# A fused attention, soft MoE and product layer on one Trainium2 core: one instruction plan for all queues, the last batch pair by pair, and memory handed on in blocks

## The chip, the cores and the metric

The kernel runs on one core of a Trainium2 chip. The metric is the device time of one execution in microseconds. The core has TensorE (PE), VectorE (DVE), ScalarE (ACT), GpSimd (POOL) and SyncE (SP), which here issues nearly all DMAs.

## The reference

```python
# attention, 8 batches x 8 heads, 576 tokens, head dimension 64; block-causal mask with blocks of 64
scores = scale * np.matmul(q, k.transpose(0, 1, 3, 2))
scores = np.where(block_i >= block_j, scores, -1e9)
attn = softmax(scores); x = attn @ v            # x becomes 4608 x 512
# soft MoE, 8 experts with 4 slots each (32 slots)
logits = x @ phi
slot_input = softmax(logits, over tokens).T @ x
slot_out[e] = np.maximum(slot_input[e] @ w1[e], 0) @ w2[e]      # w1: 512 x 1024, w2: 1024 x 512
y = softmax(logits, over slots) @ slot_out
# product layer
h = (y @ u1) * (y @ u2) @ w3                    # u1, u2: 512 x 1024, w3: 1024 x 1024
out = h @ w_out                                 # 1024 x 512
```

## The kernel before, in words

*Attention.* Heads are worked in 32 pairs (`n`), four to a batch, eight batches (`b`). For a pair, raw q and k are loaded (`op_ld`) and split into a high part (ACT, `op_cast`) and a low part (POOL, `op_sub`); a first product on TensorE (`op_M`, L360) gives block maxima by VectorE (`op_R`, L364), which a transposition and a DMA bring to a row; then come the scores (`op_Q`, L400), their exponentials on ACT (`op_E`), sums on POOL (`op_P`, for the last pair partly on VectorE) and TensorE (`op_SU`, L449), and the product with v (`op_V`, L433). After four pairs of a batch the sums are inverted and spread by DMA, x is scaled on POOL (`op_sx`), and the batch's logits, maxima, exponentials and its share of the slot inputs follow (`op_lg` to `op_SSu`). Between these, 26 pieces of 64-bit weights (`op_b`) are converted to 32 bits: w_out, the first row of w3, u1 and u2.

*What sets the order.* `Plan` (L74) lists every operation with its engine, a duration, what it waits for, PSUM banks and a due time (`OFF`, `EARLY`); `order()` plays it forward, with a look-ahead per engine (`LOOK`, `WAIT`), and returns one order. In the attention all five queues are issued in that order by hand (`manual_schedule`, L801).

*The last batch.* `push_tail` (L629) writes the chain of batch 7 after the plan: transposed sums, logits, their transpositions and reductions (`logit_t`, L664), natural x (`x_nat`, L707), dispatch maxima and exponentials (`disp_max`), slot inputs (`slot_in`, `slot_sum`, `slot_share`, `slot_T`, L737). Between the steps `fill` issues matmuls of zeros (`warm`, L42; `WARM` gives 10, 11, 16 and more). Batch 6's last steps (`S`, `cT`) are moved into this chain (`late`).

*Experts and joined weight.* `Rest.run` (L899) multiplies w3 and w_out into one weight W (8 row blocks of 24 matmuls, `w_rows`, L930), with each operand split into two terms: 192 matmuls. Pieces of w3 are loaded and converted (`convert`, `narrow`, `split`). For each expert: first layer (L1020), copy, transposition, relu, second layer (L1048); expert weights come in 16 halves of 2 MB through five windows (`load_expert`), four of them loaded late in attention. `w_steps` puts a listed number of W matmuls (`MM`) between the expert's steps. Only PE and SP are in hand order here (`MAN`); other queues are put in order by the framework. All this starts after the slot inputs: the high parts of w_out wait for `keep["shared"]` (L991).

*H and the last stage.* The experts' output is multiplied with u1 and u2 (L1089) and transposed; slot products (`slot_products`, L1108) are made on VectorE, with three small ones on POOL (L1125), and multiplied with W to H (`h_chunk`, L1131). `final` (L1173) goes over 12 groups of 384 tokens: products of combine weights (VectorE, ACT, POOL), then three tiles of 13 matmuls with H (L1238), a copy and a store.

*Memory.* Each stage opens pools and closes them; a pool of the next stage lies where an earlier one was.

Of the kernel before, what the change touches and what calls it, by code (L numbers as in the profile page):

```python
# [21 lines left out]
W3B = 4  # L22
ROT = 2
MAN = ('SP', 'PE')
ORDERED = ('PE', 'DVE', 'Activation', 'Pool', 'SP')
FIN = (7, 11, 11)
W3_AT = (0, 1, 2, 3, 4, 5, 6, 7)
SEQ = 1
WARM = (6, 10, 11, 0, 16, 0, 0, 0)
WF = 25  # L30
AHEAD = 36
HP = False
CT = (1, 2)
STEPS = 28
MM = (0, 5, 4, 13, 5, 4, 14, 5, 4, 13, 5, 4, 14, 5, 4, 13, 5, 4, 14, 5, 4, 14, 5, 4, 2, 2, 4, 3)
# [6 lines left out]
def warm(nc, keep, ps, n, w=128):  # L42

    for _ in range(n):
# [3 lines left out]
OFF = dict(ld=(-4301.23, -2731.05, -1243.02, -2278.38), ldv=(-837.82, -354.76, -2206.4, 3323.43),  # L48
           cast=(1436.93, 2916.25, 4127.87, 4251.94), sub=(1093.58, 2437.56, 2911.79, 2136.83),
           M0=(-241.73, -208.33, -267.44, -225.64), M1=(-181.87, -161.12, -221.47, -182.7),  # L50
           M2=(-125.55, -213.98, -277.53, -169.18), M3=(-174.43, -248.18, -245.29, -165.8),
           l2=(-2688.49, -1287.55, -164.78, -407.62), mT=(-95.52, -54.96, -153.52, -108.93),
           Q0=(70.48, 17.42, 44.17, 27.42), Q1=(77.27, 40.94, 76.16, 33.83), Q2=(79.67, 53.58, 68.7, 55.24),
           Q3=(105.69, 63.33, 61.76, 48.73), P0=(-834.24, 503.41, -1466.49, -981.16),
           P3=(-556.87, -58.4, -1879.82, -1649.01), V1=(194.34, 208.98, 190.03, 181.31),
           V0=(197.16, 107.82, 112.76, 86.16), SU=(190.93, 192.56, 146.47, 96.52), r=663.9, sx0=2177.73, sx1=439.67,
           sx2=-483.43, sx3=2006.86, lg=382.92, lgT=453.88, cm=2119.0, cT=699.85, LTm=-88.35, dn=468.38, xn0=451.85,
           xn1=469.47, xn2=419.96, xn3=437.32, xn4=454.2, S=587.84, b=1015.73)
EARLY = dict(M=(-1406.78, -994.39, -488.06, -373.68), m=(-997.99, -729.92, -303.75, 0.12), Q=(-585.47, -387.45, 0.93, -1.1))
PERIOD = 100.0  # L60
LOOK = dict(PE=0.0, DVE=1160.641, ACT=933.474, POOL=419.253, SP=567.979)
# [12 lines left out]
class Plan:  # L74
# [95 lines left out]
    def order(self):  # L170
# [12 lines left out]
        while len(out) < len(ops):  # L183
            best = None
            for e, R in ready.items():
                can = []
                for k in R if e != "PE" else [k for k in list(row)[:1] if k in R]:
# [3 lines left out]
                    if t < INF:  # L191
                        can.append((t, k))
# [52 lines left out]
class Attn:  # L245
# [1103 lines left out]
```

## Time and profile before

| | us |
|---|---|
| median of 3 runs | 576.44 (575.87 to 579.41) |
| profiled execution | 577.33 |
| its span, first to last instruction | 575.5 |
| TensorE busy in the span | 554.7 |

The profile is one execution. Matmuls are pipelined and their ends are modelled, so a busy TensorE is not one at its peak. A row of the timeline gives start, duration, engine, line, operation, output and inputs, a count where instructions are merged, and in brackets the idle time before it with what ended it. The granted clock is a share of 2.4 GHz; 0.50 is 1.2 GHz.

### The profile page before, as it was taken

How to read it: one execution, taken by the hardware profiler on the slowest of the kernel's cores; microseconds unless marked ns; L12 is line 12 of the kernel's file. 1: busy time of each engine (PE TensorE's matmuls, PEld its weight loads, DVE VectorE, ACT ScalarE, POOL GpSimd, SP SyncE). 2: the span in 40 equal slices, each digit the busy share in tenths (PEclk: the TensorE clock that was granted, in tenths of full speed). 3: DMA queues.
4: the chain of work that ended last, by engine and by line, in shares of the span. 5: the costliest groups of instructions: out<-in, count | busy, mean ns of one | idle time of the engine just before them, and what ended most of it. 6: DMA issues, size and time to landing. Idle time of an engine off the chain costs nothing.

```text
span 575.5 us, 13898 instructions
## 1 busy us (share of the span) xinstructions
PE 554.7 (96%) x5470; PEld 418.6 (73%) x5470; DVE 397.6 (69%) x701; ACT 321.4 (56%) x625; POOL 336.5 (58%) x246
## 2 busy tenths in 40 slices
PE   6999999999999999999999869999999999999997
PEld 3887778787887787878878545565656778888885
DVE  6678798888988979889832548652619987647550
ACT  4656668586686686876855235423433453535441
POOL 6887897978979979889776019212532122313220
PEclk9899999999999999999999978999999989999999
DMA  7255666566547365665276647999904047564732
GB/s 250 90 179 187 208 251 225 160 204 210 169 168 225 119 225 161 205 208 170 80 237 216 267 165 303 409 421 426 412 10 151 14 135 234 175 230 161 234 122 109
DMA packets 39193, 116.96 MB, mean 203 GB/s; under 512 B 5324, under 2 KB 15548, under 8 KB 37064
## 3 DMA queue, kind: packets, MB, share of 16 engines
q1 hardware_dynamic: 38948, 116.00, 58.0%
q8 instruction: 43, 0.70, 0.5%
q14 instruction: 22, 0.18, 0.1%
q10 hardware_dynamic: 180, 0.07, 0.0%
HBM read 105.75 MB, written 10.45 MB: 202 GB/s over the span
## 4 chain that ended last, share of the span: by engine, by line
PE 87%; DVE 8%; DMA 2%; ACT 2%; issue 1%; ACTq 0%; DVEq 0%
PE ps L400 19%; PE ps L1238 18%; PE ps L433 15%; PE ps L938 6%; PE ps L360 5%; PE ps L449 4%; PE ps L557 3%; PE ps L1048 3%; PE ps L1020 3%; PE ps L500 2%; PE ps L606 2%; PE ps L1240 1%; DVE bm L364 1%; DMA win<-in_moe_w 1%; DVE g_stage L1116 1%; PE ps L45 1%
## 5 line engine op out<-in xcount | busy, mean ns | idle before, releaser
L364 DVE TENSOR_REDUCE bm<-ps 128x10 f32<-128x640 f32 (+2 forms) x128 | 122.2, 987 | 33.5 <-PE ps L360 23.8
L400 PE MATMUL ps<-set 64*128 64x320 f32 (+4 forms) x1152 | 112.7, 304 | 0.5 <-ACT PTb L408 0.4
L400 PEld LDWEIGHTS ps<-set 64*128 64x128 f32 x1152 | 89.8, 186 | 5.5 <-issue 1.6
L1238 PE MATMUL ps<-H,Ph 128*128 128x512 f32 x288 | 91.5, 400 | 1.7 <-DVE H L1145 1.7
L348 POOL TENSOR_TENSOR set<-raw,set 128x1152 fp32r<-128x1152 f32 x32 | 84.9, 2657 | 8.2 <-ACT set L341 7.0
L1213 POOL TENSOR_TENSOR Pl<-rot,Ph 128x384 fp32r<-128x384 f32 x24 | 29.9, 1263 | 90.7 <-ACT Ph L1211 90.7
L418 POOL TENSOR_TENSOR acc<-PTa,PTb 128x640 f32<-128x640 f32 x32 | 49.9, 1558 | 35.8 <-ACT PTb L408 26.5
L1238 PEld LDWEIGHTS ps<-H,Ph 128*128 128x128 f32 x288 | 55.0, 191 | 15.6 <-DVE H L1145 2.1
L400 PE MATMUL ps<-shift 64*128 64x320 f32 (+4 forms) x384 | 58.5, 299 | 0.0
L1238 PE MATMUL ps<-H,Pl 128*128 128x512 f32 x144 | 57.4, 399 | 0.0
L1241 ACT COPY o<-ps 128x512 f32<-128x512 f32 x36 | 21.1, 587 | 57.3 <-PE ps L1240 56.8
L938 PE MATMUL ps<-wo,w 128*128 128x512 f32 x192 | 51.5, 409 | 0.0
L418 POOL TENSOR_TENSOR acc<-acc,PTc 128x640 f32<-128x640 f32 x31 | 48.3, 1556 | 2.0
L408 ACT ACTIVATE PTa<-ps 128x1024 f32<-128x1024 f32 x32 | 32.9, 1027 | 27.9 <-PE ps L400 22.9
L360 PE MATMUL ps<-set 64*128 64x320 f32 (+4 forms) x384 | 46.5, 317 | 0.3 <-ACT set L344 0.2
L938 PEld LDWEIGHTS ps<-wo,w 128*128 128x128 f32 x192 | 34.3, 190 | 16.8 <-issue 9.6
L442 ACT COPY xT<-ps 128x320 f32<-128x320 f32 (+1 forms) x64 | 25.5, 399 | 36.7 <-PE ps L437 28.2
L408 ACT ACTIVATE PTc<-ps 128x640 f32<-128x640 f32 (+1 forms) x64 | 39.8, 651 | 8.1 <-PE ps L400 8.1
L433 PE MATMUL ps<-PTc,v 128*64 128x320 f32 (+1 forms) x256 | 43.6, 419 | 0.0
L491 POOL TENSOR_TENSOR xT<-xT,shift 128x576 f32<-128x576 f32 x28 | 39.5, 1423 | 0.0
L1210 DVE TENSOR_TENSOR rot<-rot,crep 128x384 f32<-128x384 f32 x48 | 34.7, 755 | 5.9 <-DMA rot<-cs 5.2
L341 ACT CAST set<-raw 128x1152 fp32r<-128x1152 f32 x31 | 35.6, 1150 | 3.6 <-DMA raw<-in_qk 3.6
(234 smaller groups left out, 1115.3 us busy)
## 6 DMA issues: line engine op xcount, KB each, us to landing
win<-in_moe_w SPq DMA_DIRECT2D x16, 2048.0 KB
raw<-in_qk SPq DMA_DIRECT2D x32, 576.0 KB
v<-in_v SPq DMA_DIRECT2D x32, 320.0 KB
rot<-cs SPq DMA_DIRECT2D x48, 192.0 KB
out<-o SPq DMA_DIRECT2D x11, 768.0 KB
raw<-in_moe_w SPq DMA_DIRECT2D x16, 512.0 KB
shift<-rr SPq DMA_DIRECT2D x56, 144.0 KB
w3raw<-in_w3T SPq DMA_DIRECT2D x14, 512.0 KB
```

The lines of the kernel that those rows point to most:

```text
L341: self.nc.scalar.copy(hi, self.raw[n])
L348: self.nc.gpsimd.tensor_tensor(lo, self.raw.pop(n), hi.bitcast(F32), op=ALU.subtract)
L360: self.nc.tensor.matmul(ps[:, h, o:o + kn], lhsT=qh[r, q0:q0 + 128], rhs=kh[r, k0:k0 + kn], start=True, stop=True)
L364: self.nc.vector.tensor_reduce(self.bmb[n % 2][:, :, o:o + m // 64], self.st.pop(("M", n, i))[:, :, 0:m].rearrange("p h (n k) -> p h n k", ...
L400: self.nc.tensor.matmul(ps[:, h, o0:o0 + w], lhsT=lt[r, k] if i < 3 else lt[r], rhs=rt[r, q0:q0 + w], start=i == 0, stop=i == 3)
L408: self.nc.scalar.activation(out=out, in_=ps[:, :, 0:sum(g[3] for g in self.UNITS[u])], func=AF.Exp, scale=SCALE)
L418: eng.tensor_tensor(acc[:, :, lo:hi], a, b, op=ALU.add)
L433: mm(ps[64 * h:64 * h + 64, q0 - lo:q1 - lo], lhsT=v[:, 128 * j + 64 * h:128 * j + 64 * h + 64], rhs=pt[:, h, o:o + q1 - q0], start=j == 0 ...
L491: self.nc.gpsimd.tensor_tensor(x, x, self.rb[:, i], op=ALU.mult)
L938: nc.tensor.matmul(p, lhsT=a[:, o], rhs=b, start=c + i == 0, stop=c == 7 and i == 2)
L1210: nc.vector.tensor_tensor(p, p, crep, op=ALU.mult)
L1238: nc.tensor.matmul(ps, lhsT=a[:, k, r], rhs=b[:, k], start=n == 0, stop=False)
```

## The change

One `Plan` now holds all work up to the first slot product; all engines are issued in hand order from the first pair to the last store. `LATE`, `TAIL` and `POST` give due times for the last batches, the last batch's chain and the experts, and `OFF`, `EARLY`, `LOOK` and `WAIT` have new numbers. `op_W`'s 192 matmuls are fillers: `order()` takes one when it ends before the next due matmul can start. The chain of the last batch goes by pair. Pools are replaced by tagged blocks (`new`) that one use hands to the next. H and the last stage are written out by hand.

```diff
-WARM = (6, 10, 11, 0, 16, 0, 0, 0)
+WARM = 6
...
+    def last(self, N):
...
+        for i in range(2):
+            op("ts", i, "PE", .33, [("sb", N - 2 + i)], 1, due=f"ts{i}")
+            op("tr", i, "DVE", .5, [("ts", i)] + [("tr", 0)] * i, free="ts", due=f"ts{i}", late=.1)
+        for p in range(NP_B):
+            n = N - NP_B + p
+            op("lp", p, "PE", .55, [("c1", n), ("c0", n)] + ..., 1, mode="cols", due=f"lp{p}")
+            op("lc", p, "ACT", .36, [("lp", p)] + [("lt", p - 2)] * (p > 1), free="lp", due=f"lp{p}", late=.1)
+            op("lt", p, "PE", .33, [("lc", p)], 1, due=f"lt{p}")
+            op("lr", p, "DVE", .48, [("lt", p), ("tr", p // 3)] + [("la", p - 1)] * (p > 0), free="lt", due=f"lr{p}")
+            op("la", p, "DVE", .27 if p == 0 else .5, [("lr", p)] + [("la", p - 1)] * (p > 0), due=f"lr{p}", late=.1)
+            op("xp", p, "PE", .545, [("lp", p)], 2, due=f"xp{p}")
+            op("xv", p, "DVE", .95, [("xp", p), ("tr", p // 3)], free="xp", due=f"xv{p}")
+        op("l4", 0, "ACT", .2, [("la", 3)], due="chain")
+        op("md", 0, "PE", .25, [("la", 3), ("l4", 0)], 1, due="chain", late=.05)
+        op("mX", 0, "DVE", .65, [("md", 0), ("LTm", B - 1)], due="chain", late=.1)
...
+        op("sC", 0, "DVE", .25, [("sT", 0)], free="sT", due="chain", late=.85)
...
+        op("z6", 0, "SP", 1.15, [("z5", 0)], lat=3, due="comb", late=.5, load=.4)
+        op("z7", 0, "SP", .5, [("z6", 0), ("cTd", B - 1)], lat=3, due="comb", late=.6, load=1.)
+
+    def experts(self, N):
...
+        free = {i: pair(N - 2 + i // 3) for i in range(6)}
+        free[6] = [("ts", 1), ("lt", 2), ("LTe", B - 1), ("lgT", B - 1)]
+        free[7] = [("lt", 3), ("la", 3), ("cTd", B - 1)]
+        out = {0: [("sub", N - 2)], 1: [("sub", N - 1)], 2: [("V0", N - 3), ("V1", N - 3)], 3: [("pl", 0), ("pl", 1)],
+               **{c: [("mI", 0), ("ws", 0)] for c in range(4, 8)}}
...
+            op("wl", i, "SP", .4, win[i] if i in win else [(("L1", "L2")[(i - 5) % 2], (i - 5) // 2)], lat=2.5, load=4.85)
...
+        order = [(f, j) for g in (0, 12) for f in range(4) for j in range(g, g + 12)] + [(f, j) for f in range(4, 8) for j in range(24)]
+        for n, (f, j) in enumerate(order):
...
+            if n >= 192 - HELD:
+                deps += [("L2", 7)]
...
+            op("W", 24 * f + j, "PE", .213, deps, int(j == 0), filler=True, due="W")
...
+        for e in range(8):
+            op("L1", e, "PE", 1.87, [("wl", 2 * e), ("sC", 0)] + at(e - 1, "L2"), 1, mode="quarters", due="L", late=100. * e)
...
+            op("L2", e, "PE", 1.85, [("re", e), ("wl", 2 * e + 1)], int(e == 0), mode="quarters", due="L", late=100. * e + 40)
...
@@ order
-                for k in R if e != "PE" else [k for k in list(row)[:1] if k in R]:
+                for k in R if e != "PE" else [k for k in (*list(row)[:1], *list(fill)[:1]) if k in R]:
...
+                if e == "PE" and len(can) == 2:
+                    can = can[1:] if can[1][0] + ops[can[1][1]]["dur"] <= can[0][0] + SLIP else can[:1]
...
+    def op_lr(self, p, _):
+        r = self.tl([128, 5, 8], "r")[:, :, 2 * p:2 * p + 2].unsqueeze(3).to_broadcast([128, 5, 2, 32])
+        self.nc.vector.tensor_tensor(self.lr, self.st["lt", p][:, 0:320].rearrange("p (c h s) -> p c h s", c=5, h=2), r, op=ALU.mult)
+
+    def op_la(self, p, _):
+        L = self.keep["L"]
+        if p:
+            self.nc.vector.tensor_tensor(L, L, self.lr[:, :, 0], op=ALU.add)
+        self.nc.vector.tensor_tensor(L, L if p else self.lr[:, :, 0], self.lr[:, :, 1], op=ALU.add)
...
+        for f in range(8):
+            if f:
+                self.slot_product(f, 0)
+                self.low(f - 1)
+                self.slot_product(f, 1)
+                self.op_Gc(f, None)
+            if f == 2:
+                nc.vector.tensor_tensor(G16[:, :, 0:16], AT[:, :, 0:16], BT[:, :, 16:32], op=ALU.mult)
...
+            if f in (1, 2, 3, 4, 5, 6):
+                for i in ((0, 1), (2,)):
+                    for k in range(4):
+                        h_chunk(k, f - 1, i)
+            if f == 6:
+                for i in range(8):
+                    h_last(i)
+                nc.scalar.copy(X, Hp[4])
+        self.low(7)
+        mul(0, 0)
+        mul(0, 1)
+        for k in range(4):
+            for f in (6, 7):
+                h_chunk(k, f)
...
+        for u in range(n_u):
+            load(u + 2)
+            if u == 0:
+                for k in range(5):
+                    for t in range(3):
+                        product(u, t, k)
...
+        with tc.manual_schedule(engines={getattr(mybir.EngineType, e) for e in ORDERED}):
+            attn.run()
+            rest.run(out)
```

In the plan, `n1` to `n4` convert a piece of w3 on VectorE, `ph` and `pl` split it, `wh` and `wo` split w_out, `We` copies a row block of W out, `wM` to `wr` are `slot_sum` and `slot_share`, `mD` to `mU` the last slot inputs.

## Rows read from the trace of the kernel before

**Rows 1.** the page's part 1, busy time, share and instructions of the engines

```profile
PE 554.7 (96%) x5470; PEld 418.6 (73%) x5470; DVE 397.6 (69%) x701; ACT 321.4 (56%) x625; POOL 336.5 (58%) x246
```

**Rows 2.** by stretch: engines' busy us (x instructions), clock, DMA share, GB/s

```profile
240.00:250.00 10.00, 10.00 (x115) 8.60 (x115) 7.81 (x11) 8.45 (x19) 6.53 (x5) 1.00 0.69 224
...
319.00:330.00 11.00, 8.82 (x76) 5.51 (x72) 6.49 (x12) 2.65 (x8) 0.16 (x1) 0.96 0.66 254
...
330.00:345.00 15.00, 10.02 (x65) 7.01 (x63) 6.55 (x20) 4.66 (x15) 1.94 (x2) 0.73 0.39 150
...
345.00:350.00 5.00, 4.72 (x35) 2.38 (x36) 4.58 (x10) 4.47 (x10) 5.00 (x5) 0.53 0.51 193
...
360.00:365.00 5.00, 4.15 (x28) 2.02 (x27) 4.64 (x7) 2.52 (x6) 1.80 (x2) 1.00 0.96 370
...
365.00:417.00 52.00, 51.78 (x400) 30.79 (x402) 23.79 (x35) 18.30 (x38) 16.16 (x14) 1.00 1.01 422
...
430.00:440.00 10.00, 9.05 (x46) 5.64 (x45) 9.49 (x17) 3.85 (x10) 3.98 (x4) 1.00 0.68 215
...
460.00:470.00 10.00, 8.43 (x30) 6.76 (x31) 9.91 (x16) 4.67 (x10) 2.87 (x3) 0.83 0.36 108
```

**Rows 3.** timeline of TensorE and VectorE, end of attention to the slot inputs

```profile
328.83 2.10 PE L45 MATMUL ps<-zeros 128*128 128x128 bf16 x21 [0.97 <-DVE lr L671]
...
337.80 1.14 PE L45 MATMUL ps<-zeros 128*128 128x128 bf16 x9
...
338.94 0.79 PE L45 MATMUL ps<-zeros 128*128 128x128 bf16 x7
...
342.98 1.92 PE L742 MATMUL ps<-sel,sn 128*128 128x32 f32 x8 [0.77 <-DVE sn L739]
...
344.94 0.29 DVE L743 COPY siT<-ps 128x128 f32<-128x128 f32 x1 [2.01 <-PE ps L742]
```

**Rows 4.** timeline, expert stage and after: groups that repeat, at either clock

```profile
345.28 3.64 PE L1020 MATMUL ps<-win,siT 128*32 128x256 f32 x32 [0.38 <-DVE siT L743]
...
367.35 1.93 PE L1020 MATMUL ps<-win,siT 128*32 128x256 f32 x32
...
372.43 1.92 PE L1048 MATMUL ps<-win,win 128*32 128x512 f32 x16 [0.22 <-ACT win L1039]
...
423.00 0.97 PE L976 MATMUL ps<-sel,sos 128*128 128x32 f32 x8
...
361.50 0.69 DVE L842 SCALAR_TENSOR_TENSOR ps<-w3raw,ps 128x512 int32<-128x512 int32 x1
...
447.88 11.04 PE L1135 MATMUL ps<-W,g_stage 128*128 128x512 f32 x48
```

**Rows 5.** chain of waits in order of time, the last stage

```profile
461.57 8.57 PE ps L1238 x29
...
480.86 2.79 PE ps L1238 x12
...
568.91 2.80 PE ps L1238 x12
```

**Rows 6.** the page's part 6: size of one expert half's load

```profile
win<-in_moe_w SPq DMA_DIRECT2D x16, 2048.0 KB
```

**Rows 7.** waits of the SP queue, 300 to 440 us

```profile
SPq L892 <- DMA cs<-cT: 2.3, 1, 2.3
```

**Rows 8.** timeline: POOL and VectorE side by side at the slot products

```profile
435.34 1.70 POOL L897 TENSOR_TENSOR W<-wO,W 128x512 fp32r<-128x512 f32 x1 [1.30 <-ACT W L896]
...
435.81 1.78 DVE L1116 TENSOR_TENSOR g_stage<-g_stage 128x512 f32<-128x512 f32 x1
...
439.53 0.68 DVE L1116 TENSOR_TENSOR g_stage<-g_stage 128x512 f32<-128x512 f32 x1
```

**Rows 9.** timeline of the start: filling matmuls ahead of the second pair

```profile
13.46 2.72 PE L45 MATMUL ps<-zeros 128*128 128x256 bf16 x12 [2.30 <-DVE bm L370]
```

**Rows 10.** the page's part 5: the largest group of VectorE

```profile
L364 DVE TENSOR_REDUCE bm<-ps 128x10 f32<-128x640 f32 (+2 forms) x128 | 122.2, 987 | 33.5 <-PE ps L360 23.8
```

More of the change, by code (lines that the diff above doesn't have):

```diff
@@ new lines, in start @@
+    def start(self):
+        warm(self.nc, self.keep, self.bank((0,)), WARM, 512)
+        self.constants()
+    def run(self):
+        for (name, n), slot, idle in Plan(self.nb).order():
+            if idle > .5 and (name[0] in "MQ" or name == "mT") and n < 2:
+                warm(self.nc, self.keep, self.bank(slot), int(4.5 * idle - 1), 256)
+            f = getattr(self, "op_" + name, None) or getattr(self.rest, "op_" + name, None)
+            if f:
+                f(n, slot)
+            else:
+                f = getattr(self, "op_" + name[:-1], None) or getattr(self.rest, "op_" + name[:-1])
+                f(n, slot, int(name[-1]) if name[-1].isdigit() else name[-1])
@@ new lines, in op_We, with op_Wh, op_Wl, hq @@
+    def op_We(self, f, _):
+        self.W[f] = self.wO[:, f]
+        self.nc.scalar.copy(self.W[f], self.st["W", f])
+    def op_Wh(self, f, _):
+        self.w_terms[f] = self.two(self.attn.new(f"s{2 * f % 8}", F32R))
+        self.split(*self.w_terms[f], self.W[f], 0)
+    def op_Wl(self, f, _):
+        self.split(*self.w_terms[f], self.W[f], 1)
+    def hq(self, i):
+        return self.attn.tcw[:, 256 * (i % 2):256 * (i % 2) + 256]
+    def op_L1(self, e, slot):
+        hp, w = self.attn.bank(slot), self.weights(2 * e)
+        self.st["hp"] = hp
+        for dc in range(4):
+            for g in range(4):
+                self.nc.tensor.matmul(hp[32 * g:32 * g + 32, 0:256], lhsT=self.keep["siT"][:, dc], rhs=w[:, dc, 256 * g:256 * g + 256],
+                                      start=dc == 0, stop=dc == 3)
@@ new lines, in op_L2, with s2, op_so, op_sS @@
+    def op_L2(self, e, slot):
+        if e == 0:
+            self.st["so"] = self.attn.bank(slot)
+        w = self.weights(2 * e + 1)
+        for f in range(8):
+            g = f % 4
+            self.nc.tensor.matmul(self.st["so"][32 * g:32 * g + 32], lhsT=self.hT[e][:, f], rhs=w[:, f], start=e == 0 and f < 4, stop=e == 7 and f >= 4)
+    def s2(self):
+        return self.attn.tcw[:, 512:1024]
+    def op_so(self, i, _):
+        self.nc.scalar.copy(self.s2(), self.st["so"])
+    def op_sS(self, i, slot):
+        p = self.st["sS"] = self.attn.bank(slot)
+        for dc in range(4):
+            self.nc.tensor.matmul(p[:, 32 * dc:32 * dc + 32], lhsT=self.s2()[:, 128 * dc:128 * dc + 128], rhs=self.keep["sel32"], start=True, stop=True)
@@ new lines, in op_sd, with op_ab @@
+    def op_sd(self, i, _):
+        self.nc.vector.tensor_copy(self.hq(0)[:, 0:128], self.st["sS"][:, 0:128])
+    def op_ab(self, i, slot):
+        ab = self.st["ab"] = self.attn.bank(slot)
+        soT = self.hq(0)[:, 0:128].rearrange("p (a b) -> p a b", a=4)
+        for dc in range(4):
+            for g in range(4):
+                w = self.wA if g < 2 else self.wB
+                f = 512 * (g % 2)
+                self.nc.tensor.matmul(ab[32 * g:32 * g + 32], lhsT=soT[:, dc], rhs=w[:, dc, f:f + 512], start=dc == 0, stop=dc == 3)
```

1134 lines of the change are left out of this document (545 added, 589 removed).

## The prediction, before the change was run

> **What bounds the kernel now.** I read the page's part 1 first: TensorE is busy for 554.7 of 575.5 us [rows 1]. So the question is only which of its time can go. The table by stretches answers it, and there the reader is to look at two columns, TensorE's busy time and the granted clock. In the attention a stretch of 10 us holds 10.00 us of TensorE at clock 1.00, the level of 2.4 GHz [rows 2]: nothing idles there, and the change removes none of its matmuls. From 319 to 350 the picture breaks: 8.82 of 11, 10.02 of 15 and 4.72 of 5 us, with the clock at 0.96, 0.73 and 0.53, the last almost all at 1.2 GHz [rows 2]. That is the last batch's chain (sums, logits, maxima, exponentials, slot inputs), in which each small matmul waits for VectorE or ScalarE. The timeline of that stretch shows that part of even this busy time is zeros matmuls put in only to keep the engine going [rows 3]. From 365 to 417 TensorE is at 51.78 of 52 us, while the DMA engines are at share 1.01 and 422 GB/s [rows 2]: two resources are full at once. Smaller holes stand at 360 to 365, 430 to 440 and 460 to 470 [rows 2]. The chain of waits in order of time then shows the last stage as an even row of tiles [rows 5].
>
> **The change part by part.** The sum is a count of TensorE's time between 319.0 and the first tile of the last stage, because the order of everything else is rebuilt and only that engine is full. What can go:
>
> 1. Idle time in the chain: 2.18 + 4.98 + 0.28 = 7.44 us [rows 2].
> 2. The zeros matmuls behind the opening ones (21, 9 and 7 of them): 2.10 + 1.14 + 0.79 = 4.03 us [rows 3]. The change deletes them; only the start keeps its own.
> 3. Matmuls at the low clock: the first expert's first layer takes 3.64 us and a later one 1.93 [rows 4], 1.71 too much; eight 128x32 matmuls of the slot inputs take 1.92 us [rows 3], and eight of the same shape 0.97 later [rows 4], 0.95 too much. Together 2.66 us. Other pieces of the chain will be slow too; I leave them uncounted.
> 4. Holes at 360 to 365 (0.85) and 430 to 440 (0.95): 1.80 us; the hole ahead of the last stage, 1.57 us [rows 2].
> 5. The first six tiles of the last stage. A tile's period is (568.91 - 480.86) / 29 = 3.036 us; the six between 461.57 and 480.86 took 19.29 instead of 18.22 us: 1.07 us [rows 5]. The clock there is 0.83 [rows 2].
>
> The sum is 7.44 + 4.03 + 2.66 + 1.80 + 1.57 + 1.07 = 18.6 us. It can only go if useful work stands where the holes were. The joined weight gives that: 192 matmuls W at 11.04 / 48 = 0.230 us each [rows 4], 44 us in all, which so far start only after 348 and now may run, as fillers, as soon as their operands exist. Their cover is thus what I check stage by stage.
>
> *The chain.* Holes and zeros matmuls make 7.44 + 4.03 = 11.5 us to be filled, less what the chain by pair takes out by itself (three of the four pairs' logits, sums and transposes now lie under attention; only the last pair's stay). Of W, the half rows that need no block of the last batch are 48, or 11.0 us. But each half row needs a converted piece of w3: four VectorE operations of 0.69 us [rows 4], 2.8 us a piece, and five pieces must be converted before all 48 are ready. VectorE has in 319 to 345 13.0 us busy of 26 [rows 2], with the chain's work among it. So at least the first 12 (no conversion left) and likely 24 to 36 (5.5 to 8.3 us) are there in time. Cover lies between 2.8 and 11.0 us; the need shrinks by a few us because the chain is shorter. I take 1.0 us as left idle, with ends 0 and 6.2 (9.0 us of need in 330 to 345 and its zeros, less 2.8).
>
> *The experts.* When the slot inputs are there, TensorE has 8 x (1.93 + 1.92) = 30.8 us of layers [rows 4] and, of W, 192 less 24 done less the 30 that the plan holds back, 138 x 0.230 = 31.7 us: 62.5 us. Beside it eleven expert halves and four to eight pieces of w3 (a quarter of a half each) must come. A half is 2048 KB [rows 6], 2.10 MB, 4.97 us at 422 GB/s [rows 2]: 11 x 4.97 + 4 to 8 x 1.24 = 59.6 to 64.6 us, after the first layer's 1.93 us has freed a block and with the last half's 1.92 us behind it: 63.5 to 68.5 us. The two are about equal, transfers longer by 1 to 6 us. Before, one more half and six more pieces lay in this stretch; they move ahead of the slot inputs, where the DMA share is 0.66 and 0.39 [rows 2]. I take 1.5 us of stall, near the lower end because four of the pieces need only half rows of W that are done early. The plan also puts both writes of the last batch's weights on SP, the second waiting for the first to land; behind it on SP stand the experts' loads. Such a wait cost a load 2.3 us before [rows 7]; with its five blocks loaded ahead this is covered, at worst it adds those 2.3.
>
> *The end of the experts, H and the last stage.* The 30 held matmuls (6.9 us) stand in the gaps between copies, transposes and slot products; the low part of a slot product comes a step later and the first tile of the last stage is taken piece by piece over three tiles, so that it needs only a quarter of H. Three small products move from POOL to VectorE. I take 0.8 us as left (0 to 2.5: the 0.95 and 1.57 holes return).
>
> *Adds on VectorE.* The logits are now summed by adds with both inputs in SBUF, beside POOL's subtractions. An add took 1.78 us while POOL ran such a subtraction from 435.34 on, and 0.68 us without [rows 8]: 1.1 us for one meeting. Two such adds of the last pair lie in the chain: 0 to 2.2 us, I take 0.5. The Trainium skill (SBUF — State Buffer, Who interferes with whom) says that a VectorE instruction with two SBUF inputs contends with a GpSimd one that reads SBUF, and that the second to come blocks entirely. By it either engine may be the one that waits, and with every meeting lost the sum would be 1.7 us poorer than mine; the trace agrees with the rule at 1.78 against 0.68.
>
> *Start and attention.* The start's plan is new. Twelve zeros matmuls stand there for 2.72 us ahead of the second pair's transposition [rows 9]; between -1 and +2.7 us may go, I take +0.5. In the attention the same matmuls come in a slightly other order on a full engine: 0, between -1.5 and +1.5. Memory passed on in blocks moves nothing itself: no instruction of it is on the path, and where the block is late it is a wait already counted.
>
> So 1.0 + 1.5 + 0.8 + 0.5 = 3.8 us stay of the 18.6, and 0.5 is won at the start: a gain of 15.3 us. The profiled execution took 577.33 us (span 575.5 and 1.8 around it); it becomes 562.0. The median of the runs is 0.9 below it: **561.1 us**.
>
> **Rivals.**
>
> *The transfers bind.* For it: DMA share 1.01 already [rows 2]. Against: more is loaded ahead. With all eight pieces behind the slot inputs and the wait on SP, 6.0 + 2.3 us stall instead of 1.5; the gain is 8.5, the time 567.9.
>
> *The clock and the cover fail.* If only 12 matmuls W are ready in the chain, 6.2 us instead of 1.0 stay idle, and the low clock's 2.66 us stay too: gain 7.4, time 569.0. For it: even with 37 zeros matmuls the clock is 0.73 and 0.53 [rows 2], and these are now gone. Against: VectorE is half idle there. The Trainium skill (TensorE: Matmul & The Clock Gate, What's actually happening) says that the throttled state is the default and that activity lifts it, which speaks against deleting matmuls that only warm; by it the time would be this case's.
>
> *Everything closes.* All 18.6 go, and 2.72 + 0.5 at the start: gain 21.8, time 554.6. For it: W is 44 us of work that fits any hole. Against: the first layers wait for transfers.
>
> *Slower.* The attention's queues are in a fixed order, and with new due times one reduction of VectorE (0.987 us [rows 10]) comes too late in each pair's turn, so that TensorE waits for its bank. Over 28 pairs that is 27.6 us: 588.7. It decides from 15.3 / 28 = 0.55 us a pair. Against: TensorE idles 0.00 in that stretch, with VectorE at 7.81 of 10 [rows 2].
>
> **How the numbers follow.** The forecast has 0.56 (own range 556 to 566), the transfers 0.14, clock and cover 0.10, everything closes 0.13, slower 0.07. The range of 552 to 570 holds the first, second and fourth and most of the third, with the bounds of start and attention at its lower end. A measurement of this kernel tells about 1%, 5.8 us, from no change. Faster by over 1% (below 570.7): 0.86, the first, second and fourth and a third of clock and cover. Within 1%: 0.08, the rest of that and a little of the slower case. Slower by over 1%: 0.06.
>
> **What would show it.** Right: no zeros matmuls after the start; W beginning before the slot inputs; slot inputs 10 to 15 us earlier; the clock near 1.00 throughout; the last stage's first tile near 446 with a period of 3.036 us. Wrong: a new idle on TensorE behind expert loads (the second case), a clock below 0.8 in the chain (the third), or a batch of attention that takes longer than before (the slower case). The forecast falls if the last stage's first tile starts after 453 or before 440.

## The result, and the profile after

The changed kernel takes 570.39 us (median of 7, 568.34 to 572.36) against 576.44: ratio 0.9887, interval 0.9859 to 0.9914. Run once more later (after_again) it gave 569.94, ratio 0.9879 (0.9860 to 0.9897). So it is faster by 1.1%, some 6.5 us where I forecast 15.3. The profiled execution took 569.49, against 577.33: 7.84 us less. The reading below accounts for these 7.84.

Where they stand is seen in four marks. The kernel before, timeline of TensorE (last expert's second layer; first product of H) and the stage of the experts by window:

```profile
420.11 1.92 PE L1048 MATMUL ps<-win,win 128*32 128x512 f32 x16
...
434.09 1.92 PE L1141 MATMUL ps<-wO,g_stage 128*32 128x512 f32 x16 [0.95 <-POOL g_stage L1127]
```

```profile
345.28:422.03 76.75, 75.68 (x570) 43.41 (x570) 41.56 (x62) 29.34 (x62) 33.49 (x27) 0.97 0.91 372
```

The changed kernel, the same marks in the timeline of TensorE, with what delayed them (L1066 is a product of the joined weight, L1087 and L1108 the experts' layers, L1224 H, L1287 the last stage):

```profile
337.39 1.93 PE L1087 MATMUL ps<-win,siT 128*32 128x256 f32 x32 [0.28 <-DVE siT L889]
...
346.34 1.17 PE L1066 MATMUL ps<-raw,s 128*128 128x512 f32 x4 [2.15 <-DVE vt L1046]
...
349.05 2.81 PE L1108 MATMUL ps<-win,win 128*32 128x512 f32 x16
...
390.09 0.44 PE L1096 MATMUL ps<-ident,tc 128*128 128x128 f32 x2 [0.49 <-ACT tc L1091]
392.32 1.22 PE L1066 MATMUL ps<-wx,s 128*128 128x512 f32 x2 [1.79 <-ACT s L983]
393.52 3.64 PE L1108 MATMUL ps<-win 128*32 128x512 f32 x16
397.09 3.31 PE L1066 MATMUL ps<-wx,s 128*128 128x512 f32 x10
...
409.10 1.92 PE L1108 MATMUL ps<-win,win 128*32 128x512 f32 x16
...
427.17 11.27 PE L1224 MATMUL ps<-g_stage 128*128 128x512 f32 x48 [0.68 <-ACT wO L1070]
...
453.17 6.67 PE L1287 MATMUL ps<-H,pA 128*128 128x512 f32 x28
```

The changed kernel by window, columns as in [rows 2]:

```profile
240.00:250.00 10.00, 10.00 (x118) 8.66 (x118) 7.78 (x11) 8.28 (x17) 6.38 (x5) 1.00 0.65 219
319.00:330.00 11.00, 10.99 (x97) 8.95 (x98) 9.79 (x30) 6.38 (x20) 2.72 (x3) 1.00 1.00 398
330.00:340.00 10.00, 9.22 (x82) 5.75 (x80) 8.88 (x23) 5.49 (x14) 5.38 (x5) 1.00 0.72 286
...
460.00:470.00 10.00, 9.55 (x36) 6.65 (x37) 9.05 (x16) 6.61 (x13) 3.96 (x3) 1.00 0.44 139
...
337.39:411.02 73.63, 68.40 (x527) 36.60 (x527) 34.51 (x52) 24.62 (x52) 22.01 (x19) 0.93 0.93 380
...
346.00:352.00 6.00, 5.66 (x26) 2.54 (x26) 4.32 (x8) 2.97 (x6) 2.56 (x2) 0.72 1.01 426
...
392.40:400.40 8.00, 8.00 (x29) 3.72 (x30) 6.79 (x10) 1.63 (x3) 2.50 (x2) 0.61 1.00 418
...
340.00:410.00 70.00, 65.26 (x489) 35.30 (x492) 31.05 (x46) 22.28 (x48) 18.38 (x16) 0.93 0.96 394
```

The experts' first layer starts 345.28 - 337.39 = 7.9 us earlier. From there to the end of the last second layer the stage takes 73.63 instead of 76.75 us: 3.1 won. From that end to the first product of H it takes 16.15 (411.02 to 427.17) instead of 12.06: 4.1 lost. From there to the last tile, 568.91 [rows 5] before and 561.00 after, 134.82 and 133.83: 1.0 won. The sum is 7.9.

The chain came out as hoped: 319 to 330, which held 8.82 us of work [rows 2], holds 10.99 of 11 at clock 1.00, and 24 of the 192 products W stand ahead of the slot inputs, with no zeros matmul. From 319.01 to 337.39 only 0.28 us are idle. But the stage of the experts should then have shrunk far more. It holds 124 W instead of 167 (24 lie ahead, 44 instead of 25 behind). At the 0.268 us that a W took between the layers before (38.6 us for 144), the 43 are 11.5 us, and the first layer no longer takes 3.64 [rows 4] but 1.93: 13.2 us, of which 3.1 came. Of the 10.1 that are missing, 4.2 are new idle time (5.23 against 1.07 us) and, by an estimate from the rows above, 4 to 5 are low clock: in the two stretches behind the holes it is 0.72 and 0.61 (between 0.50, the 1.2 GHz, and 1.00, the 2.4), so 6.00 x 0.28 + 8.00 x 0.39 = 4.8 us of clock are missing, and a layer of 1.92 us takes 2.81 and 3.64 there. That leaves 1 to 2 us that I can't place.

Who is late? The first hole (at 344) ends with VectorE's unpacking of a piece of w3, the second (at 391) with ScalarE's split of piece 9. VectorE, the changed kernel's timeline, and the chain of waits in order of time:

```profile
345.51 0.69 DVE L1046 SCALAR_TENSOR_TENSOR vt<-vt,ps 128x512 f32<-128x512 bf16 x1
...
388.64 0.69 DVE L1040 TENSOR_SCALAR ps<-s 128x512 int32<-128x512 int32 x1 [32.16 <-DMA s<-in_w3T]
```

```profile
367.50 21.05 DMA s<-in_w3T
```

At 345 VectorE comes straight from the chain and the last batch's weights to be written out, at 8.88 of 10 busy from 330 to 340. At 388 it has idled 32 us for piece 9: that piece is asked for only at 367.50, when a block is free, and lands 21.05 us later, with the DMA engines at share 1.0. Pieces 8 to 15 are the late ones: each waits for a block that W has to leave. Only piece 8 is asked for ahead of the slot inputs, when 12 W have run:

```profile
331.08 0.33 SPq L1020 DMA_DIRECT2D s<-in_w3T  x1
```

The other seven come behind them, and so does piece 7, which waits for a block of the last batch. The changed kernel's DMA issues from 336 to 412 us:

```profile
win<-in_moe_w SPq DMA_DIRECT2D x9, 2048.0 KB
s<-in_w3T SPq DMA_DIRECT2D x8, 512.0 KB
xw<-in_moe_w SPq DMA_DIRECT2D x2, 2048.0 KB
```

11 x 2.10 + 8 x 0.52 = 27.3 MB, at 422 GB/s 64.6 us. Two theories follow. *Transfers:* these bytes are the wall. *Unpacking and order:* VectorE's unpacking, and the order in which pieces and steps wait for each other, are. The rival to both is that TensorE's work is the whole of it.

### The profile page after: what moved, and what is told of

The parts are those of the page before. It is cut to its first block, busy times and chain, and to the rows that moved or that the text cites. A ratio compares the mean times of both kernels' runs of the same rounds, so it can differ in the third digit from the quotient of the medians.

```text
span 567.6 us, 13929 instructions
## 1 busy us (share of the span) xinstructions
PE 550.2 (97%) x5444; PEld 414.3 (73%) x5444; DVE 393.6 (69%) x716; ACT 320.9 (57%) x624; POOL 334.1 (59%) x242
## 4 chain that ended last, share of the span: by engine, by line
PE 85%; DMA 6%; DVE 4%; ACT 2%; POOL 1%; issue 1%; DVEq 0%; POOLq 0%; ACTq 0%; SPq 0%
PE ps L542 20%; PE ps L1287 16%; PE ps L575 15%; PE ps L1066 6%; PE ps L502 5%; PE ps L591 4%; DMA s<-in_w3T 4%; PE ps L1224 3%; PE ps L697 3%; PE ps L1108 2%; DMA raw<-in_qk 2%; PE ps L640 2%; PE ps L1289 1%; PE ps L746 1%; PE ps L1087 1%; PE ps L518 1%
## 5 line engine op out<-in xcount | busy, mean ns | idle before, releaser
L506 DVE TENSOR_REDUCE tc<-ps 128x10 f32<-128x640 f32 (+2 forms) x128 | 122.5, 987 | 33.4 <-PE ps L502 25.8
L550 ACT ACTIVATE s<-ps 128x1024 f32<-128x1024 f32 (+2 forms) x128 | 102.9, 838 | 44.7 <-PE ps L542 34.5
L560 POOL TENSOR_TENSOR tc<-tc,s 128x384 f32<-128x384 f32 (+1 forms) x63 | 80.7, 1281 | 7.0 <-ACT s L550 3.6
L560 POOL TENSOR_TENSOR tc<-s,s 128x640 f32<-128x640 f32 x32 | 49.9, 1560 | 30.4 <-ACT s L550 24.0
L575 PE MATMUL ps<-s,xw 128*64 128x320 f32 (+3 forms) x528 | 63.7, 383 | 0.0
L1287 PE MATMUL ps<-H,pB 128*128 128x512 f32 x216 | 53.7, 395 | 0.4 <-POOL pB L1267 0.4
L1287 PE MATMUL ps<-H,pA 128*128 128x512 f32 x216 | 53.2, 395 | 0.2 <-DVE H L1331 0.2
L1287 PEld LDWEIGHTS ps<-H,pB 128*128 128x128 f32 x216 | 40.6, 189 | 10.7 <-POOL pB L1267 1.1
L1287 PEld LDWEIGHTS ps<-H,pA 128*128 128x128 f32 x216 | 40.6, 188 | 10.3 <-DVE H L1331 0.5
L542 PEld LDWEIGHTS ps<-shift 64*128 64x128 f32 x384 | 36.8, 187 | 0.5
```

The costliest lines, as they stand in the source:

```text
L506: self.nc.vector.tensor_reduce(self.bmb[n % 2][:, :, o:o + m // 64], self.st.pop(("M", n, i))[:, :, 0:m].rearrange("p h (n k) -> p h n k", ...
L542: self.nc.tensor.matmul(ps[:, h, o0:o0 + w], lhsT=lt[r, k] if i < 3 else lt[r], rhs=rt[r, q0:q0 + w], start=i == 0, stop=i == 3)
L550: self.nc.scalar.activation(out=out, in_=ps[:, :, 0:sum(g[3] for g in self.UNITS[u])], func=AF.Exp, scale=SCALE)
L560: eng.tensor_tensor(acc[:, :, lo:hi], a, b, op=ALU.add)
L575: mm(ps[64 * h:64 * h + 64, q0 - lo:q1 - lo], lhsT=v[:, 128 * j + 64 * h:128 * j + 64 * h + 64], rhs=pt[:, h, o:o + q1 - q0], start=j == 0 ...
L1287: nc.tensor.matmul(ps, lhsT=a[:, k, r], rhs=b[:, k], start=k + i == 0, stop=False)
```

## Experiments

Ratios are to the kernel before, run beside each. "Stage" is the time from the first expert's first layer to the start of the last second layer (changed kernel: 409.10 - 337.39 = 71.7).

### Half the bytes; late pieces on another queue; no early W; no hand order at the end

**a_half.** Half of expert halves 5 to 15 is left out.

```diff
+        n = (4 if first else 8) // (2 if i > 4 else 1)
-        self.nc.sync.dma_start(out=v, in_=self.io["moe_w1" if first else "moe_w2"][i // 2].rearrange("p (c f) -> p c f", c=4 if first else 8))
+        self.nc.sync.dma_start(out=v[:, 0:n], in_=self.io["moe_w1" if first else "moe_w2"][i // 2].rearrange("p (c f) -> p c f", c=4 if first else 8)[:, 0:n])
```

> Leaves out half of each expert half from the sixth load on (the stale half of the block is multiplied instead), 11.5 MB or 27 us of transfers at 422 GB/s; all instructions stay. The changed kernel took 570.4 us. If transfers (their amount or their order) pace the experts, the second layer of the last expert ends near 401 instead of 411.0 and the time is 560 to 563. If TensorE's own work and its fixed order pace them, less than 2 us are won: 568.5 or more.

565.46, ratio 0.9809 (0.9777 to 0.9840); stage 68.4. Some 5 us, between the two numbers: bytes are part of it, but both holes are still there, the second with 1.56 us instead of 1.79. The timelines of VectorE and of ScalarE in this run show why:

```profile
383.19 0.69 DVE L1041 TENSOR_SCALAR ps<-s 128x512 int32<-128x512 int32 x1 [27.08 <-ACT wO L1071]
...
390.83 0.69 DVE L1047 SCALAR_TENSOR_TENSOR vt<-vt,ps 128x512 f32<-128x512 bf16 x1 [5.49 <-ACT vt L1031]
```

```profile
389.81 0.37 ACT L1092 COPY tc<-ps 128x256 f32<-128x256 f32 x1 [2.05 <-PE ps L1088]
390.08 0.67 ACT L1031 ACTIVATE vt<-s 128x512 bf16<-128x512 f32 x1
```

Piece 9 is there at 383, but its fourth step waits 5.49 us for a square (L1031). ScalarE's hand order puts that square behind the copy of the seventh expert's first layer, for which ScalarE itself idles 2.05 us. An order that fits late data holds up early data. So of the second hole only some 0.2 us hang on the piece. What differs more is the clock behind it: the layer that took 3.64 us takes 1.92 here. Whether that is the bytes' doing is taken up below the table.

**b_actq.** The late pieces are asked for on ScalarE's queue.

```diff
-        self.nc.sync.dma_start(out=self.w3_t[i], in_=self.io["w3T"][i // 2, i % 2])
+        (self.nc.scalar if i > 7 else self.nc.sync).dma_start(out=self.w3_t[i], in_=self.io["w3T"][i // 2, i % 2])
```

> The last eight pieces of w3 are issued on ScalarE's queue instead of SP's; the bytes stay the same. Theory order (pieces stand behind 2 MB halves in one queue, 21 us from issue to landing, and W and what is behind it on TensorE wait): pieces land within 8 us, the idle at 390 to 393 and the low clock there go, 3 to 5 us won, 565.5 to 567.5. Theory amount (27.3 MB after the slot inputs pace the layers in any order): within 1 us of 570.4.

576.91, ratio 1.0013 (0.9988 to 1.0038): 6 us worse than the changed kernel, neither theory's number. The edit put a new wait on the path. ScalarE and its queue in this run:

```profile
393.81 0.33 ACTq L1020 DMA_DIRECT2D s<-in_w3T  x1
394.19 0.58 ACT L1070 COPY wO<-ps 128x512 f32<-128x512 f32 x1 [8.81 <-DMA win<-in_moe_w]
395.71 0.27 ACT L909 COPY tc<-ps 128x128 f32<-128x128 f32 x1
```

ScalarE's copies stand 8.81 us behind an issue that can't start, and the next expert's first layer waits 5.0 us for the last row (L910 with it). The issue's block is free from 385.4 on, when 96 W have run. By the chain of waits, it starts when an expert half on SP's queue lands (365.39 + 28.33 = 393.72):

```profile
365.39 28.33 DMA win<-in_moe_w
```

Why it waits for that landing is not shown. The run tells nothing of queues as such.

**c_nofill.** The first W waits for the slot inputs.

```diff
+            if n == 0:
+                deps += [("sC", 0)]
```

> No matmul of W before the slot inputs (24 of them, 5.5 us, move behind). If TensorE paces the experts, the time grows by those 5.5 us less what the chain wins: 573 to 576. If transfers pace them, TensorE takes the 24 into its idle time: less than 2 us, 570 to 572.5. Slot inputs at 337 if the fillers stand only in waits, 2 us or more earlier if they delay the chain.

574.08, ratio 0.9958 (0.9932 to 0.9984), in the range set for TensorE pacing the experts: the early W are worth 3.7 us of medians. But TensorE is not all that paces them: it also waits 2.5 us for an expert half at 393. Windows of this run:

```profile
320.00:330.00 10.00, 7.91 (x71) 6.01 (x69) 8.83 (x29) 6.33 (x20) 2.19 (x3) 1.00 0.99 406
330.00:340.00 10.00, 7.64 (x67) 4.11 (x67) 9.62 (x22) 4.33 (x11) 6.38 (x5) 0.83 0.44 174
```

The chain's holes are back (7.91 and 7.64 of 10) and the clock is 0.83, but the first layer starts at 335.37, 2.0 us earlier. Half of that lies ahead of the chain, which begins at 318.03 instead of 319.01 in this execution; 1.0 us is what the W between the chain's steps delay it. The stage is 72.4 and ends little earlier than with the early W (407.74 against 409.10).

**d_auto.** H and the last stage are ordered by the framework, as before the change.

```diff
-            rest.run(out)
+        rest.run(out)
```

> H and the last stage are put in order by the framework as before, the rest stays in hand order. If the hand order there is worth what I had priced (the 1.57 us hole and 1.07 us of slow tiles), the time is 572 to 573.5; the rival, that it is worth nothing, gives 570.4 within 1 us; all before the first slot product stays as it is within 0.5 us.

581.18, ratio 1.0086 (1.0060 to 1.0113), 10.8 us worse than the changed kernel and worse than the kernel before, far above both numbers. The waits of TensorE in this run begin with

```profile
PE ps L1228 <- DVE g_stage L1310: 7.3, 1, 7.3
PE ps L1066 <- ACT s L983: 3.1, 1, 3.1
```

The three small products that went from POOL to VectorE are issued late if no one writes their place down, and H waits 7.3 us. The hand order is what makes that move bearable; the change needs it.

### Taking the unpacking and the bytes away, each and both, in two orders

The second order, **e_even**, reads, unpacks and multiplies the late pieces with the even ones first, so that no block waits for the half rows that come last:

```diff
+SEQ = (0, 1, 2, 3, 4, 5, 6, 7, 8, 10, 12, 14, 9, 11, 13, 15)
...
+                q = SEQ.index(i)
-                at2 = [("b4", 25)] if i == 2 else [("n4", i - 1)]
+                at2 = [("b4", 25)] if i == 2 else [("n4", SEQ[q - 1])]
...
-        order = [(f, j) for g in (0, 12) for f in range(4) for j in range(g, g + 12)] + [(f, j) for f in range(4, 8) for j in range(24)]
+        order = [(f, j) for F in (range(4), range(4, 8)) for g in (0, 12) for f in F for j in range(g, g + 12)]
```

> The eight late pieces of the weight are read, converted and multiplied with the even ones first (8, 10, 12, 14, then 9, 11, 13, 15), and the products of the joined weight's second half go in that order. Theory 'order' (a late piece waits in the ring of blocks for a product that itself waits for the last piece of the other matrix, so piece 9 is asked for at 367.5 and lands at 388.55 behind expert halves, and VectorE idles 32 us): the hole of 1.8 us and the low clock (0.66) at 390 to 400 go, 3 to 5 us less than the changed kernel's 570.4: 565 to 567. Theory 'bytes' (27 MB follow the slot inputs, whatever their order): the last byte still lands at 405 to 407, the holes move to experts or to the end, 569 to 571.

**g_light** leaves two of the four VectorE steps of each unpacking out, in the change's order:

```diff
+        if step in (2, 3):
+            return
```

> Steps 2 and 3 of the unpacking of the weight's pieces 2 to 15 are left out (28 VectorE instructions of 0.70 us, 19.6 us of VectorE; the weight so made is not the reference's), the order of the rest and all transfers stay. Theory 'VectorE' (pieces 2 to 4 are converted too late since VectorE is 0.9 busy from 320 to 350 with the chain of the last batch between them): the hole of 2.2 us at 344 and its low clock (0.85, 0.9 us) go, and 1.4 us of the 1.8 at 391: 3 to 4.5 us less than the changed kernel, 566 to 567.5. Theory 'bytes': pieces 5 and 9 wait for transfers anyway, only the hole at 344 shrinks, and what is won comes back at 390: 568.5 to 570.5.

**h_light_half** joins it with half the bytes; **i_light_even** and **j_even_half** put each, **r_even_light_half** both into the even order.

> Both the lighter unpacking (steps 2 and 3 left out for pieces 2 to 15) and half the bytes of expert halves 5 to 15 (the experts' results so made are not the reference's). If VectorE's unpacking and the transfers are the whole of what stands between the changed kernel and the sum of its TensorE work: 559 to 562. If a third thing stands there (ScalarE's hand order, in which the square of piece 9 stands behind the copies of expert 5): 563 to 565, with the hole at 390 of over 1 us still there and its wait on ScalarE.

> The even pieces first and the lighter unpacking (steps 2 and 3 left out for pieces 2 to 15), full transfers. Theory 'order and VectorE' (the two together make nearly all of the lost time, bytes little): 561 to 563.5. Theory 'bytes': 566 or more, with waits of experts on their halves (win or xw <- DMA) over 2 us in sum.

> The even pieces first, and half the bytes of expert halves 5 to 15 left out (the experts' results so made are not the reference's). With full transfers the even order gave 567.6 and the last expert's second layer started at 408.07, against 409.10 in the changed kernel; with half the bytes alone 565.5 and 406.02. Theory 'transfers pin the end of the experts': without them that layer comes at 403 to 404.5, and with 30 instead of 44 products behind it the time is 561.5 to 564. Theory 'TensorE or the converting paces the experts in this order too': that layer stays above 406.5 and the time above 565.5.

> The even pieces first, the lighter unpacking (steps 2 and 3 left out for pieces 2 to 15) and half the bytes of expert halves 5 to 15 (neither the weight nor the experts so made are the reference's). In the even order the bytes alone gave nothing (568.3) and the unpacking alone 1.4 us (566.2). Theory 'two walls of nearly one height, unpacking and transfers, each of which hides the other': both together give more than the sum, the last expert's second layer starts at 403 to 405, the time is 562 to 564.5. Theory 'TensorE's own work is the wall in this order': 565.5 or more, that layer above 406.

| | us | ratio (interval) | stage, us |
|---|---|---|---|
| changed kernel | 570.39 | 0.9887 (0.9859 to 0.9914) | 71.7 |
| after_again (the same kernel) | 569.94 | 0.9879 (0.9860 to 0.9897) | 69.0 |
| g_light | 570.75 | 0.9894 (0.9862 to 0.9925) | 73.0 |
| a_half | 565.46 | 0.9809 (0.9777 to 0.9840) | 68.4 |
| h_light_half | 563.14 | 0.9774 (0.9746 to 0.9803) | 66.3 |
| e_even | 567.60 | 0.9851 (0.9834 to 0.9868) | 69.8 |
| i_light_even | 566.17 | 0.9821 (0.9801 to 0.9841) | 70.3 |
| j_even_half | 568.27 | 0.9854 (0.9804 to 0.9904) | 69.3 |
| r_even_light_half | 563.66 | 0.9771 (0.9751 to 0.9791) | 65.5 |

A stage is read from one profiled execution, and these differ. The changed kernel was profiled twice. The second time it took 566.31 us, the fastest of its 13 runs; TensorE at the second hole, and the window 340 to 410:

```profile
391.10 0.73 PE L1066 MATMUL ps<-wx,s 128*128 128x512 f32 x2 [1.56 <-ACT s L983]
392.29 1.92 PE L1108 MATMUL ps<-win 128*32 128x512 f32 x16 [0.45 <-DMA win<-in_moe_w]
```

```profile
340.00:410.00 70.00, 65.33 (x506) 36.64 (x498) 32.40 (x47) 25.07 (x52) 21.13 (x18) 0.98 0.95 391
```

With the same instructions and all bytes the layer takes 1.92 us, and the stage 69.0. Against this profile a_half's stage is 0.6 us shorter and e_even's 0.8 longer, so the stage alone tells neither from the changed kernel. The medians do for a_half, 4.5 to 4.9 us with intervals apart; for e_even, 2.3 to 2.8 us, the intervals still overlap. How much of the bytes' gain comes through the clock behind the second hole is open. The stages of h_light_half and r_even_light_half lie below both profiles.

In the window 340 to 410 the count of TensorE's instructions (in brackets behind its busy time) tells the same as the stage; the changed kernel has 489 in the first profile. g_light:

```profile
340.00:410.00 70.00, 62.38 (x478) 34.36 (x476) 15.04 (x22) 21.11 (x46) 18.20 (x15) 0.95 0.94 390
```

e_even:

```profile
340.00:410.00 70.00, 66.60 (x513) 37.56 (x509) 32.14 (x47) 22.57 (x49) 20.24 (x16) 0.98 0.95 391
```

j_even_half:

```profile
340.00:410.00 70.00, 67.06 (x521) 37.68 (x514) 34.33 (x51) 22.51 (x50) 20.30 (x17) 0.98 0.69 246
```

r_even_light_half:

```profile
340.00:410.00 70.00, 70.00 (x549) 39.97 (x545) 14.81 (x23) 24.45 (x52) 23.77 (x21) 1.00 0.64 238
```

Unpacking alone is taken away in g_light: the hole at 344 is gone, VectorE falls from 31 to 15 us, and nothing is won, since TensorE now waits for expert halves; the time is 0.25 us above the range set for the bytes. Its waits:

```profile
PE ps L1110 <- DMA win<-in_moe_w: 2.7, 3, 1.4
PE ps L1068 <- ACT s L983: 1.9, 1, 1.9
PE ps L1089 <- DMA win<-in_moe_w: 1.4, 1, 1.4
```

i_light_even does the same in the even order and falls in the range set for the bytes, with these waits (its profile, 568.91 us, is the slowest of its five runs):

```profile
PE ps L1112 <- DMA win<-in_moe_w: 3.4, 3, 2.0
```

Bytes alone are taken away in j_even_half: DMA falls from 391 to 246 GB/s, and nothing is won either (568.27 against 567.60), since the unpacking's hole of 2.2 us and its low clock stay. Time and layer (407.93) are those set for TensorE or the converting. Both away: 70.00 of 70 us busy, clock 1.00, 549 instructions, 3.9 us won, where the two alone give 1.4 and -0.7; the time is as set for two walls, the last layer (401.67) even earlier than its 403. The interval of r_even_light_half lies apart from those of e, i and j. That both give more than the sum is not clear from the medians, where 3.2 us stand against some 3.4 of noise by the four intervals. The profiles show it: with the unpacking lighter, the hole at 344 comes back as waits for halves (4.1 us in g_light, 3.4 in i_light_even); with half the bytes no half is waited for, but the hole stays; with both, neither is there. So the walls are real and stand at nearly one height: each hides the other. In the change's order bytes count by themselves (4.9 us). h_light_half still has the wait on ScalarE, 1.55 us ahead of 386.66, as the second case of its expectation had it, and with 563.14 its time.

e_even's own gain is 2.8 us of medians, less than 3 to 5: the hole at 392 is gone and 30 instead of 44 W are left behind the experts, but that leaves the steps behind them bare.

### A faster version?

**k_even_comb** is the even order with the first edit below, **p_tail** with the next two, **q_tail_comb** with all three, **s_all22** is q with `HELD` at 22 instead of 30, **after_again** the changed kernel.

```diff
-        op("z1", 0, "DVE", .6, [("la", 3)], due="comb")
+        op("z1", 0, "DVE", .6, [("la", 3), ("n4", 5)], due="comb")
...
-            op("gh", f, "ACT", .55, [("We", f), ("L2", 5 if f < 2 else 7)], due="gh", late=10. * f)
+            op("gh", f, "ACT", .55, [("We", f), ("L2", 5) if f < 2 else ("so", 0)], due="gh", late=10. * f)
...
-                op("Wl", f, "POOL", 1.26, [("Wh", f)], due="Wh", late=10. * f)
+                op("Wl", f, "POOL", 1.26, [("Wh", f)] + [("G", 0)] * (f > 5), due="Wh", late=10. * f)
```

> The even pieces first, and the last batch's weights to be written out (3.7 us of VectorE between 335 and 340) wait for the unpacking of piece 5. Theory 'transfers pin the end': the slot inputs come 0.5 to 1 us earlier, the hole of 2.2 us at 344 closes, and the last expert's second layer starts only as much earlier as the slot inputs do: 566 to 567.5, with what the hole gave back seen as waits for expert halves. Theory 'VectorE': the closed hole counts in full: 563.5 to 565.

> The even pieces first, and behind the experts two orders changed: ScalarE copies the experts' sum before it splits two rows of the weight (1.05 us ahead of that copy at 410.09), and POOL's last two low parts wait for the first slot product (beside them VectorE's steps took 1.14 instead of 0.20 and 1.78 instead of 0.69). With the even order the tail of 14.2 us from the last expert to the first product of H is a chain of small steps, not TensorE's work (holes of 1.96, 0.71 and 0.23 us). If that chain is what binds there: 1.5 to 2.5 us less, 565 to 566. If TensorE's work binds: 567 to 568.

> All three: the even pieces first, the written-out weights after the unpacking of piece 5, and the two changed orders behind the experts. If the transfers pin the end of the experts and the chain behind them the start of H, the two add up: 564 to 565.5. If VectorE's unpacking counts in full too: 561.5 to 563.

> As the run with the three edits of order together (even pieces first, written-out weights after piece 5's unpacking, two orders behind the experts; 565.8), and 22 instead of 30 products of the joined weight held back until the experts end. There TensorE waited 2.0 us for the last expert half with no product left to run, the clock fell, and the chain behind left a hole of 0.9 us in spite of 30 products. If the held products are that spare work: hole and low clock go, 0.5 to 2 us less, 563.5 to 565.3. If the chain behind the experts binds without them: 565.5 to 567.

> The changed kernel unaltered, on the same chip as the run before it, so that the two can be compared without a change of chip: 569.5 to 571.0 if the time of the first comparison holds (0.9887 of the kernel before); the version with four edits of order is faster than it by over 4 us if its gain is real.

k: 568.59, 0.9864 (0.9806 to 0.9922): the hole at 344 closes and comes back as 2.7 us of waits for halves, one of 2.1 before the last layer, as the transfers' theory had it (a little above its number). p: 566.95, 0.9853 (0.9795 to 0.9911): the first product of H waits 1.1 instead of 2.0 us, as the order on ScalarE had moved, while POOL still met the first product (a step of 1.16 for 0.20 us); unclear against e_even. q: 565.76, 0.9812 (0.9768 to 0.9856), a quarter of a us above the range set for the sum of the two. s: 568.17, 0.9850 (0.9830 to 0.9870), a miss: the wait for the last half is gone, but with 22 W the chain behind the experts lies bare, as this row of its TensorE timeline shows:

```profile
423.59 13.71 PE L1226 MATMUL ps<-g_stage 128*128 128x512 f32 x48 [3.63 <-ACT g_stage L1208]
```

H starts hardly earlier (423.59; q 423.80), and 13.71 us for what takes 11.27 above is the low clock behind a hole of 3.63. On the same chip after_again had 569.94, 1.8 us above s, with intervals that overlap; only q, on another chip, lies over 4 us below it. The five versions with the even pieces first lie at 0.981 to 0.986, against 0.988 to 0.989: all faster than the kernel before. They lie 1.4 to 4.6 us below the changed kernel's medians, but only q's interval is apart from its two (0.9768 to 0.9856; 0.9859 to 0.9914 and 0.9860 to 0.9897), and q is the best of five. A gain is likely; its size, and which version is best, are not settled.

Part of what held H up in e_even (0.9 of 2.0 us) is seen beside POOL, in the timelines of VectorE and of POOL:

```profile
422.32 1.14 DVE L1201 TENSOR_SCALAR g_stage<-g_stage 128x32 f32<-128x32 f32 x1
...
425.18 1.78 DVE L1199 TENSOR_TENSOR g_stage<-g_stage 128x512 f32<-128x512 f32 x1
427.00 0.20 DVE L1201 TENSOR_SCALAR g_stage<-g_stage 128x32 f32<-128x32 f32 x1
...
428.91 0.69 DVE L1199 TENSOR_TENSOR g_stage<-g_stage 128x512 f32<-128x512 f32 x1
```

```profile
421.85 1.56 POOL L983 TENSOR_TENSOR s<-wO,s 128x512 fp32r<-128x512 f32 x1 [6.05 <-ACT s L985]
424.72 1.70 POOL L983 TENSOR_TENSOR s<-wO,s 128x512 fp32r<-128x512 f32 x1 [1.31 <-ACT s L985]
```

A VectorE step that begins beside a running subtraction of POOL ends only after it: 1.14 us for 0.20 (423.46 against POOL's 423.41), 1.78 for 0.69 (426.96 against 426.42). The Trainium skill (SBUF — State Buffer, Who interferes with whom) says that the shared port pair is an exclusive lock and that issue order decides who blocks; the trace agrees: POOL came first both times, and VectorE waited.

## Why the prediction was wrong

**The sum of what could go was not far off.** With unpacking and bytes out of the way the time is 563.66 (r) or 563.14 (h), inside the forecast's own range of 556 to 566; in r TensorE runs 70 us without a gap. Both leave out work that the kernel needs, so they show what bound the change and not what it can reach. The 2.6 us that r misses to 561.1 are about as much as its holes behind the experts: 2.0, 0.7 and 0.2 us before the first products of H.

**The step that failed is "the experts": 1.5 us of stall.** I set 62.5 us of TensorE against 63.5 to 68.5 of transfers and took the low end "because four of the pieces need only half rows of W that are done early". Of these four one is asked for ahead of the slot inputs, since only 24 of the 48 early W had run by then; eight pieces follow behind, and piece 9 waits for a block and then 21.05 us for its bytes. And I weighed only two resources. VectorE's unpacking I weighed in the chain alone, where 24 W were indeed ready; it came up short in the next stage, in the first hole. The changed kernel's stage with its last layer is 73.63 us for 124 W; r's is 65.5 + 1.9 = 67.4 for 138. The 14 W between them are 14 x 0.262 = 3.7 us, so 73.6 + 3.7 - 67.4 = 9.9 us were lost, not 1.5. That is 8.4 more than forecast, and 15.3 - 8.4 = 6.9 is near the 7.84 won. In the second profile of the changed kernel, where the clock did not fall behind the second hole, the loss is 69.0 + 1.9 + 3.7 - 67.4 = 7.2 us. ScalarE's hand order, which holds the second hole at 1.56 us when the data is early, was in none of my accounts.

**TensorE's 62.5 was too small as well.** From 353.49 to 407.93 in j_even_half TensorE is busy throughout, and 131 W take 34.34 us: 0.262 each, not the 0.230 of an unbroken row of 48 [rows 4]. That is 138 x 0.032 = 4.4 us, and r's 67.4 is nearer to 66.9 than to 62.5. In the sum by differences it cancels; in the comparison of the two resources it made TensorE look as if it had room.

**Signs.** Right: no zeros matmuls after the start, W ahead of the slot inputs (24, worth 3.7 us by c_nofill), clock 1.00 through the chain, attention's windows unchanged (10.00 of 10 as in [rows 2]). Wrong: the slot inputs come 7.9 us earlier (8.9 in the second profile), not 10 to 15; the last stage's first product starts at 453.17, not near 446, and so past the 453 at which the forecast was to fall; the clock is 0.72 and 0.61 behind the experts' holes. The chain's 1.0 us left idle was about right (0.28); that it is filled does not make it shorter. What I had counted ahead of the first layer is 2.18 + 4.98 + 4.03 + 0.95 = 12.1 us; the 24 W that now stand there take 7.03. That leaves 5.1, and with the 0.5 that the work before the last batch ends earlier (its first sums stand at 291.5 instead of 292.0, as forecast) 5.6 of the 7.9 seen. The 10 to 15 counted the filled time as well. What W saves there is paid out only if the next stage can take it. The last pair's two adds took 0.33 and 0.32 us, so the 0.5 set for their meeting POOL was not lost.

**The end of the experts, H and the last stage: 0.8 us.** 1.0 us was won from the first product of H on, where I had counted 1.57 + 1.07; the tail ahead of it grew by 4.1, of which 19 more W (25 to 44) at 0.230 make 4.4. The plan held back 30, but the late pieces made it 44.

**The rivals.** "The transfers bind" (567.9) was half of it: eight pieces did come behind the slot inputs, but with half the bytes the time is still 565.46. "Clock and cover" (569.0) came near by its number only: its place was the chain, where clock and cover were good. The Trainium skill (TensorE: Matmul & The Clock Gate, What's actually happening) says that activity lifts the clock; by it deleting the zeros matmuls spoke against the change, and the trace shows it harmless where W took their place (clock 1.00; 0.83 in c_nofill, where none did) and the rule at work in the stage behind (0.72 and 0.61 after idle stretches). "Slower" did not come: from the third batch to the eighth, one follows the other after 38.3 to 38.6 us in both kernels.

What stays open: how much of what the bytes give comes through the clock behind the second hole; 2.3 of the 7.9 us by which the slot inputs come earlier; and 1 to 2 of the 10.1 us above.

## What to carry to other kernels

Work that fills a hole in one stage pays only if the next stage has room for what it saves: set up the balance of that stage for every engine and for the transfers, not for the two that look full. If taking one suspect away gives nothing, take the next away with it before you clear the first: two walls of one height hide each other. Profile a kernel twice before you read 3 us from one execution: two of the changed kernel differ by 2.7 in this stage. And take the price of a filler from where it stands between other work (0.262), not from an unbroken row (0.230).

## What the runs showed of the hardware

A queue in hand order turns an early arrival into no gain (5.49 us behind a square), and an issue on ScalarE's queue that can't start holds ScalarE itself (8.81 us). The clock's fall can cost as much as the hole before it, and does not come each time: behind a hole of 1.79 us (and one of 0.49 just before) the layer of 1.92 us took 3.64, and after 1.55 and 0.49 at the same place 2.98 in h_light_half; in a_half and in the changed kernel's second profile, after 1.56 and 0.49, it took 1.92.
